# One load of y as two halves on two DMA rings: an elementwise multiply-add on one core

## The chip, the core and the metric

The kernel runs on one NeuronCore of a Trainium2 chip. The metric is device microseconds (us) of one execution, as the median of several. Nearly all of the time goes into transfers by the core's 16 DMA engines (98.6% of the span in the kernel before); two rings feed them in these profiles, one filled by the SP queue (q1) and one by the ACT queue (q10).

Ratios are the mean time of one kernel's fast runs over that of the other's in the same rounds, so they are not quite the ratio of the medians quoted. On one core a run is called slow only because its time is over 1.5% above the fastest of the same kernel.

## The reference

```python
B, S, D = 1024, 16, 512          # bfloat16
def reference(x, y, gamma):      # x, y: (B, S, D); gamma: (D,)
    return x + gamma * y
```

x, y and the output are 16.8 MB each. The 16,384 rows of 512 elements lie as 128 partitions with 128 rows of 1 KB each, so that a load of "rows 0 to 64" moves one contiguous 64 KB run for each of 128 partitions.

## The kernel before

Two lists say what each ring carries, in order. `('y', a, b)` loads rows a to b of y, `('x', a, b, at)` loads rows of x into the x buffer from slot `at`, `('g',)` loads gamma, `('s', a, b)` stores.

```python
PIECES = [53, 11, 53, 11]
SP  = [('y', 0, 64), ('x', 0, 64, 0), ('y', 64, 128), ('x', 64, 117, 0), ('x', 117, 128, 64)]
ACT = [('g',), ('s', 0, 64), ('s', 64, 128)]
EARLY = (1, 0)              # so many of each list are issued ahead of the opening barrier
RELEASE = ('x', 64, 117, 0) # the stores may go once this load has landed
DVE = [('m', 0), ('m', 1), ('a', 0), ('a', 1), ('m', 2), ('m', 3), ('a', 2), ('a', 3)]
# ... cut: buffers; y and the results share one buffer of 128 rows, x has 75 slots ...
def ring(eng, what, n_early):
    known, went = 0, False
    for k, w in enumerate(what):
        kind = w[0]
        need = frees(w) if kind == "x" else ...     # adds that must be over before this goes (cut)
        if need > known:
            eng.wait_ge(s_add, need)
        # ... cut: the DMA itself, with its own semaphore
# gamma is spread over the partitions by a matmul with ones, and cast to bfloat16:
nc.tensor.matmul(gamma_ps, ones_row, gamma_row, start=True, stop=True).then_inc(s_ps, 1)
nc.vector.tensor_copy(out=gamma_sb, in_=gamma_ps).then_inc(s_dve, 1)
# ... cut; then, for each entry of DVE: 'm' is y = y * gamma, 'a' is y = x + y, on one piece of rows
```

The first multiply needs y's first rows **and** gamma. The load `('x', 64, 117, 0)` overwrites slots 0 to 53, so SP holds it back until the first add, of 53 rows, is done. The recorded texts, and so this document, call it "the third x load"; in SP's list it is the second of three, issued together with the third.

## Time and profile before

| | before |
|---|---|
| median of 6 runs | 120.08 us |
| span of the profiled run | 118.6 us |
| share of the span that the 16 engines' packets fill | 66.0 + 32.6 = 98.6% |
| VectorE busy | 70.0 us (59%) |
| matmul that spreads gamma starts | 9.73 us |
| first multiply / first add start | 21.94 / 41.39 us |
| third x load issued | 55.71 us |

The reading order is the shares first, then the timeline; its lines stand in the prediction. The question for every delay is whether it reaches the first point where computing feeds back into the transfers: the third x load. The stores wait for adds too, but with time to spare: the last one is issued at 95.40, and the first one's packets end at 98.3 to 98.9.

### The profile page before, as it was taken

What the parts mean: (1) busy time and instruction counts of PE and PEld (TensorE: products, weight loads), DVE (VectorE), ACT (ScalarE), POOL (GpSimd) and SP (SyncE); (2) the same over time, 40 slices, a digit from 0 to 9 for tenths busy, and PEclk for the clock granted to TensorE, in tenths of its full rate; (3) what the DMA queues carried; (4) which work ended last, traced back from release to release, by engine and by line L of the source; (5) the groups of instructions that cost most, each with busy time, mean ns of one, the idle gap of its engine ahead of it and who ended that gap; (6) DMA issues with size and microseconds to landing.
All of it is one profiled execution on the core that took longest, in us unless ns stands there. A gap on an engine that the chain in (4) does not pass through costs nothing. (4 is left out here: it accounts for less than half of the span.)

```text
span 118.6 us, 78 instructions
## 1 busy us (share of the span) xinstructions
PE 0.6 (0%) x1; PEld 0.1 (0%) x1; DVE 70.0 (59%) x10; POOL 0.2 (0%) x4
## 2 busy tenths in 40 slices
PE   0001000000000000000000000000000000000000
PEld 0000000000000000000000000000000000000000
DVE  0002000599999299999759999999999910000000
POOL 0000000000000000000000000000000000000000
DMA  9889888998899888998896969598899888988892
GB/s 354 354 376 685 354 354 354 597 464 354 354 398 663 354 354 354 663 398 354 354 586 293 586 293 567 220 639 354 354 575 486 354 354 376 685 354 354 354 619 88
DMA packets 1010, 50.33 MB, mean 424 GB/s; under 512 B 113, under 2 KB 114, under 8 KB 114
## 3 DMA queue, kind: packets, MB, share of 16 engines
q1 hardware_dynamic: 720, 33.55, 66.0%
q10 hardware_dynamic: 290, 16.78, 32.6%
HBM read 33.56 MB, written 16.78 MB: 424 GB/s over the span
## 5 line engine op out<-in xcount | busy, mean ns | idle before, releaser
L156 DVE TENSOR_TENSOR y_sb<-y_sb,gamma_sb 128x27136 bf16<-128x27136 bf16 (+1 forms) x4 | 34.6, 8688 | 12.7 <-DVEq L25 12.7
L165 DVE TENSOR_TENSOR y_sb<-x_sb,y_sb 128x27136 bf16<-128x27136 bf16 (+1 forms) x4 | 34.6, 8688 | 2.3 <-DVEq L25 2.2
L132 DVE CAST gamma_sb<-gamma_ps 128x512 bf16<-128x512 f32 x1 | 0.7, 692 | 8.8 <-DVEq L25 8.8
L127 DVE MEMSET ones_row<- 1x128 bf16 x1 | 0.2, 165 | 1.5 <-PEq L41 1.5
L130 PE MATMUL gamma_ps<-gamma_row,ones_row 1*128 1x512 bf16 x1 | 0.6, 578 | 9.7 <-PEq L25 9.7
L130 PEld LDWEIGHTS gamma_ps<-gamma_row,ones_row 1*128 1x128 bf16 x1 | 0.1, 100 | 9.7 <-issue 9.7
L194 POOL MEMSET const-uint8-127<- 128x1 uint8 x1 | 0.1, 102 | 0.0
L194 POOL MEMSET const-bfloat16-1.0<- 128x1 bf16 x1 | 0.1, 101 | 0.0
L194 POOL MEMSET const-float32-0.0<- 128x1 f32 x1 | 0.1, 98 | 0.2 <-issue 0.2
L194 POOL MEMSET const-float32-1.0<- 128x1 f32 x1 | 0.1, 98 | 0.0
## 6 DMA issues: line engine op xcount, KB each, us to landing
x_sb<-in_x_dram SPq DMA_DIRECT2D x1, 6784.0 KB, 20.8
x_sb<-in_x_dram SPq DMA_DIRECT2D x1, 1408.0 KB, 23.9
y_sb<-in_y_dram SPq DMA_DIRECT2D x2, 40.2
out_dram<-y_sb ACTq DMA_DIRECT2D x2, 22.8
x_sb<-in_x_dram SPq DMA_DIRECT2D x1, 39.7
gamma_row<-in_gamma_dram ACTq DMA_DIRECT2D x1, 1.0 KB
```

Source lines behind the costliest of these rows:

```text
L127: nc.vector.memset(ones_row, 1.0).then_inc(s_ones, 1)
L130: nc.tensor.matmul(gamma_ps, ones_row, gamma_row, start=True, stop=True).then_inc(s_ps, 1)
L132: nc.vector.tensor_copy(out=gamma_sb, in_=gamma_ps).then_inc(s_dve, 1)
L156: nc.vector.tensor_tensor(out=yt, in0=yt, in1=g, op=MULT).then_inc(s_dve, 1)
L165: nc.vector.tensor_tensor(out=yt, in0=xt, in1=yt, op=ADD).then_inc(s_add, 1)
L194: nc = _bacc.Bacc("TRN2", target_bir_lowering=False, num_devices=1)
```

## The change

The intent: both rings get work at the earliest moment, and y's first 64 rows come as two halves at once.

```diff
-SP = [('y', 0, 64), ('x', 0, 64, 0), ('y', 64, 128), ('x', 64, 117, 0), ('x', 117, 128, 64)]
-ACT = [('g',), ('s', 0, 64), ('s', 64, 128)]
+SP = [('y', 0, 32), ('x', 0, 64, 0), ('y', 64, 128), ('x', 64, 117, 0), ('x', 117, 128, 64)]
+ACT = [('y', 32, 64), ('g',), ('s', 0, 64), ('s', 64, 128)]

-EARLY = (1, 0)
+EARLY = (1, 1)
```

Gamma's load is not new, but it now stands second in its ring.

## The prediction

> **What bounds the kernel now.** I read the totals first, then the order of instructions, then the waits, then the trace's packet records (one record per transfer of a row by a DMA engine, with queue, start and duration).
>
> ```profile
> span 118.6 us, 78 instructions
> PE 0.6 (0%) x1; PEld 0.1 (0%) x1; DVE 70.0 (59%) x10; POOL 0.2 (0%) x4
> DMA packets 1010, 50.33 MB, mean 424 GB/s; under 512 B 113, under 2 KB 114, under 8 KB 114
> q1 hardware_dynamic: 720, 33.55, 66.0%
> q10 hardware_dynamic: 290, 16.78, 32.6%
> ```
>
> The two queues together fill 66.0 + 32.6 = 98.6% of 16 engines' span; VectorE is busy 59%. The DMA engines are the bound, with bytes that no reordering changes. The span can shrink only out of the 1.4% that is not filled (1.7 us: the start and the last receipt) and can grow only if the engines run dry. Of the packets 896 are data rows (7 large transfers x 128 rows), one is gamma's row of 1 KB, 113 are the small semaphore writes that end each engine's share of a transfer (7 x 16, plus one for gamma, which runs on one engine).
>
> ```profile
> 0.00 0.37 SPq L116 DMA_DIRECT2D y_sb<-in_y_dram  x1
> ...
> 1.43 0.33 SPq L113 DMA_DIRECT2D x_sb<-in_x_dram  x1
> 1.43 0.52 ACTq L110 DMA_DIRECT2D gamma_row<-in_gamma_dram  x1
> ...
> 9.73 0.58 PE L130 MATMUL gamma_ps<-gamma_row,ones_row 1*128 1x512 bf16 x1 [9.73 <-PEq L25]
> 10.46 0.69 DVE L132 CAST gamma_sb<-gamma_ps 128x512 bf16<-128x512 f32 x1 [8.78 <-DVEq L25]
> 21.94 17.29 DVE L156 TENSOR_TENSOR y_sb<-y_sb,gamma_sb 128x27136 bf16<-128x27136 bf16 x2 [10.79 <-DVEq L25]
> 41.39 17.29 DVE L165 TENSOR_TENSOR y_sb<-x_sb,y_sb 128x27136 bf16<-128x27136 bf16 x2 [2.16 <-DVEq L25]
> 55.71 0.81 SPq L113 DMA_DIRECT2D x_sb<-in_x_dram  x2
> 60.63 17.29 DVE L156 TENSOR_TENSOR y_sb<-y_sb,gamma_sb 128x27136 bf16<-128x27136 bf16 x2 [1.95 <-DVEq L25]
> ```
>
> This is the timeline: start, duration, engine, what. Gamma is ready early (cast done 10.46 + 0.69 = 11.15), so the first multiply at 21.94 waits only for y's first 64 rows. The one dependency that feeds back into the DMA stream is at 55.71: the third x load overwrites the x buffer, so SP issues it only when the first add (41.39 + 14.29 for its 53-row piece = 55.68) is done. The packet records show the SP ring still has y rows 64 to 128 to move until 59.6 to 60.0, so this issue is about 4 us early, and the ACT ring is empty then. Each 64 KB packet takes 2.42 us and they follow without a gap from about 1 us on: 16 x 65,536 B / 2.42 us = 433 GB/s.
>
> [...] Gamma was issued at 1.43 while the engine that carries it was on its first y packet (1.01 to 4.41); its 1 KB went at 6.82, between y packets two and three, and its 4-byte semaphore write at 9.28, after the third. [...] gamma, a single row, took 0.52 us when SP's x issue of 0.33 us had begun 5 ns before it. [...]
>
> **The change, part by part.**
>
> Removed: nothing. The same bytes move. The 8.4 MB y load becomes two of 4.2 MB: 128 more packets (32 KB rows instead of 64 KB) and 16 more semaphore writes of about 0.01 us. Cost under 0.1 us per engine. One more semaphore wait on VectorE, about 0.1 us.
>
> Start of the stream: first packets now begin 1.0 to 1.6 us after SP's issue and take 2.7 to 3.4 us instead of 2.42. A second ring can't start before the first did, so I give the start no gain, at most 0.3 us.
>
> Moved: gamma now stands behind y rows 32 to 64 in the ACT ring, and SP's ring goes on with x once its own half is out. Write A1..A8 and B1..B8 for one engine's packets of the halves (1.21 us each), s for a semaphore write, x1.. for x packets (2.42 us). SP issues at 0.00; ACT's first recorded instruction is at 0.13, so I expect [...] one packet committed ahead: A1 A2 B1 A3 B2 ... A8 B7 sA B8 x1 sB x2 gamma x3 sGamma. Sixteen halves take what eight full packets took, so B8 still ends at 21.36 on gamma's engine. Three x packets follow ahead of gamma's semaphore write: 21.36 + 3 x 2.42 = 28.6, and it is seen some 0.3 us later (9.28 to 9.6 before), 28.9. From gamma landed to a multiply able to start is 1.55 us (9.6 to 11.15) plus two waits, 0.2: **30.65 instead of 21.94**, 8.7 us late. y's second half lands near 24.1, no longer the last condition.
>
> How much is absorbed? The multiplies take 17.29: 30.65 + 17.29 + 0.15 (the gap a multiply-to-add wait takes, 77.92 to 78.07) = 48.1 for the first add, which had waited for x until 41.39. It ends at 62.4 and the third x load is issued then, 6.7 us later than 55.71. Its packets follow by at least 1.0 us (the first y load), 63.4; the ring ran dry at 59.6 to 60.0. The engines stand idle some 3.4 to 3.8 us, and the restart stretches the first packet by up to 0.6: **about +4.0 us**.
>
> Does the end take it back? No: x lands 4 us later, the stores start 4 us later, and they fill the DMA engines to the end. Nor does it grow: VectorE then runs unbroken to about 100.2 (48.1 + 3 x 17.29 + 0.15), and the last store, issued there, reaches the engines by about 101.2 to 101.8, ahead of the first store's last packet (98.3 to 98.6 before, 102.4 then).
>
> **Rivals.**
>
> *Even alternation.* If both rings' first packets stand ready together, the order ends A8 B8 sA sB x1 gamma x2 sGamma. Gamma is seen at 21.36 + 2 x 2.42 + 0.3 = 26.5, the multiply starts at 28.3, the third x load is issued at 60.0 and packets resume near 61.1 or later: 1.3 to 1.9 us lost, about 121.7. For it: the halves are small and issued within a fraction of a packet. Against it: [...] the packet committed ahead of gamma.
>
> *ACT gets ahead.* Then its half finishes first, gamma goes in the very next turns, the multiply starts at 22 to 25.5, and the slack of 4 us hides it: 120.1. For it: 0.13 us is little, and ACT's first record then is not a DMA. Against it: SP's issue is the first record of all.
>
> *Deeper commitment.* If what is committed ahead is counted in bytes, two 32 KB packets go before B1, four x packets go before gamma's semaphore write, and all is 2.4 us later: about 126.5. For it: the first store, issued at 76.88, found three or more 11 KB packets still going ahead of it. Against it: the store's own latency may explain that.
>
> *The start gains.* The intent: both rings feeding the engines at once. It would need idle time at the start, of which there is about 1 us before the first packet, set by one issue's latency. I see no way to 2%.
>
> **Range and chances.** SP first with one packet ahead 0.43 (about 124), deeper 0.22 (about 126.5), even 0.19 (about 121.7), ACT first 0.14 (about 120.1), something else 0.02. The 2% line is at 122.5. Slower sums to 0.65, same to 0.33. The median falls on 124.0. The range of 8 in 10 is 120.2 to 126.7.
>
> **What would show each step.** In the changed profile: ACT's y issue near 0.1 to 0.4[...]. The gamma matmul should move from 9.73 to about 29, the first multiply from 21.94 to about 30.7 with the gamma cast just before it, the third x issue from 55.71 to about 62.4, and the DMA row should show a dent of 3 to 4 us near 60 to 64, with nothing idle later. A matmul at 26.6 means even alternation, at 31.4 the deeper commitment, below 24.5 ACT first. The prediction is wrong if gamma slips past the x packets, so that the first add still starts near 41.4, or if the third x load is delayed and the ring nevertheless doesn't run dry.

That one packet goes ahead of a newcomer was the author's estimate, from gamma in the kernel before: issued from 1.43 to 1.95, it went at 6.82, behind a y packet begun at 4.41. The 0.1 us of a semaphore wait was an estimate too; in the runs, the idle time before a first multiply that gamma holds up is 0.37 us with two loads of y to wait for (the changed kernel) and 0.26 with one (one ring, gamma late).

## The result, and the profile after

The changed kernel takes **122.14 us** (121.97 to 122.37, 6 runs) against 120.08: a ratio of 1.0169, with a 95% interval of 1.0153 to 1.0184. It is slower, by less than 2%, which the record's classes call "same".

The totals of the changed kernel's page:

```profile
span 121.1 us, 80 instructions
DMA packets 1154, 50.33 MB, mean 416 GB/s; under 512 B 129, under 2 KB 130, under 8 KB 130
q1 hardware_dynamic: 720, 29.36, 57.5%
q10 hardware_dynamic: 434, 20.97, 40.0%
```

The bytes are those of before. There are 1154 - 1010 = 144 more packets, the 128 of 32 KB and the 16 semaphore writes that were counted beforehand. ACT's ring carries 4.2 MB more.

The timeline of the changed kernel (start, duration, engine, line, what):

```profile
0.00 0.37 SPq L116 DMA_DIRECT2D y_sb<-in_y_dram  x1
0.12 0.38 ACTq L116 DMA_DIRECT2D y_sb<-in_y_dram  x1
...
26.60 0.58 PE L130 MATMUL gamma_ps<-gamma_row,ones_row 1*128 1x512 bf16 x1 [26.60 <-PEq L25]
27.32 0.69 DVE L132 CAST gamma_sb<-gamma_ps 128x512 bf16<-128x512 f32 x1 [25.50 <-DVEq L25]
28.39 17.30 DVE L156 TENSOR_TENSOR y_sb<-y_sb,gamma_sb 128x27136 bf16<-128x27136 bf16 x2 [0.37 <-DVEq L25]
45.83 17.29 DVE L165 TENSOR_TENSOR y_sb<-x_sb,y_sb 128x27136 bf16<-128x27136 bf16 x2
60.15 0.80 SPq L113 DMA_DIRECT2D x_sb<-in_x_dram  x2
63.04 17.29 DVE L156 TENSOR_TENSOR y_sb<-y_sb,gamma_sb 128x27136 bf16<-128x27136 bf16 x2
```

Gamma's matmul starts at 26.60 instead of 9.73, and now it is gamma that the first multiply waits for: the cast ends at 28.01, the multiply starts at 28.39. From there VectorE has no idle time in brackets before any group: everything that had slack (2.16 us before the first add, 1.95 before the second pair of multiplies) is used up. The third x load goes out at 60.15, 4.4 us later than before.

What that does to the transfers is seen in two stretches. First the kernel before, then the changed one; the columns are the stretch, its length, the busy time of PE, PEld, VectorE and POOL with instruction counts, the clock, the DMA share, and GB/s. A packet is counted where it starts.

```profile
59.00:65.00 6.00, 0.00 (x0) 0.00 (x0) 4.37 (x1) 0.00 (x0) 1.00 1.00 434
0.00:59.00 59.00, 0.58 (x1) 0.10 (x1) 35.44 (x6) 0.20 (x4) 1.00 1.00 427
```

```profile
59.00:65.00 6.00, 0.00 (x0) 0.00 (x0) 6.00 (x3) 0.00 (x0) 1.00 0.76 289
0.00:59.00 59.00, 0.58 (x1) 0.10 (x1) 31.32 (x5) 0.20 (x4) 1.00 1.01 427
```

Up to 59 us the two kernels move the same bytes, as far as such a count can tell: it steps by whole packets, of 2.0 to 2.4 us on each engine. No gain of the two rings at the start is seen, and no loss either. Between 59 and 65 us the changed kernel moves (434 - 289) x 6 = 870 KB less, which is one packet of 53 rows less on each of the 16 engines, or **2.0 us** at 434 GB/s.

The packet records show it without such steps. They carry no engine number, but each packet's end meets the next one's start, and so they can be strung into 16 rows. Before, every engine's first packet of the third x load follows its last y packet without a gap, between 59.64 and 60.14, takes 2.00 us, and ends at 61.90 on average. After, the last y packets end at 60.23 to 60.59, the first x packets start at 61.11 to 62.53, most of them take 2.4 to 3.0 us, and they end at 64.02 on average. These 2.1 us are the whole difference of the medians (2.06): on average 0.5 because y itself ended later in this profile, 1.1 of idle time, and 0.5 of a slow first packet. (In the changed kernel's second profile, further down, y ended as before; the idle time was 1.5 and the slow packet 0.7.)

The records also show the order of the packets at the start. Write A1 to A8 for one engine's packets of SP's half, B1 to B8 for those of ACT's half. On all 16 engines the first B packet starts at 2.86 to 3.30 us, directly behind A1, and the rings go on in strict turns; gamma's 1 KB went at 23.61, and its semaphore's last count arrived at 26.46. That is A8 B8, the semaphore writes, one x packet, gamma, another x packet, gamma's semaphore write.

### The profile page after: what moved, and what is told of

The parts are those of the page before. It is cut to its first block, busy times and chain, and to the rows that moved or that the text cites. A ratio compares the mean times of both kernels' runs of the same rounds, so it can differ in the third digit from the quotient of the medians.

```text
span 121.1 us, 80 instructions
## 1 busy us (share of the span) xinstructions
PE 0.6 (0%) x1; PEld 0.1 (0%) x1; DVE 69.9 (58%) x10; POOL 0.2 (0%) x4
## 2 busy tenths in 40 slices
DMA packets 1154, 50.33 MB, mean 416 GB/s; under 512 B 129, under 2 KB 130, under 8 KB 130
## 5 line engine op out<-in xcount | busy, mean ns | idle before, releaser
L130 PE MATMUL gamma_ps<-gamma_row,ones_row 1*128 1x512 bf16 x1 | 0.6, 578 | 26.6 <-PEq L25 26.6
L130 PEld LDWEIGHTS gamma_ps<-gamma_row,ones_row 1*128 1x128 bf16 x1 | 0.1, 100 | 26.6 <-issue 26.6
```

## The experiments

Two theories stood against each other. **Late gamma**: gamma waits behind two of SP's x packets, the first multiply and the first add start late, and the third x load is issued when its ring is already empty. **Two rings**: the second ring with its smaller packets costs time by itself, and gamma's lateness is an accident. A further question was why the packets went in strict turns, and not A1 A2 B1 as the prediction had preferred. Kernels of one batch shared a chip and the runs of the kernel before (medians 119.99, 120.06 and 120.06 us in the three batches).

### Halves kept, gamma moved

```diff
-SP = [('y', 0, 32), ('x', 0, 64, 0), ...
+SP = [('y', 0, 32), ('g',), ('x', 0, 64, 0), ...
-ACT = [('y', 32, 64), ('g',), ('s', 0, 64), ('s', 64, 128)]
+ACT = [('y', 32, 64), ('s', 0, 64), ('s', 64, 128)]
```

> The changed kernel, with gamma's load moved from the ACT ring to the SP ring, right behind SP's half of y and ahead of x; the two halves stay as they are, on two rings at once. Theory 1 (the 2 us come from gamma, which waited behind two x packets, and from nothing else in the two halves): gamma's packet and its semaphore write now go without an x packet ahead of them, near 21.3 us, it is seen near 21.7, the first multiply starts near 23.4, the first add stays at its x-bound 41.4, the third x load is issued near 55.7, nothing runs dry, and the time is that of before within 0.4%: 119.9 to 120.5. Theory 2 (two rings with 32 KB packets cost time by themselves): still 121.5 to 122.5.

Measured: 120.09 us, ratio 1.0011 (0.9994 to 1.0029). Its timeline:

```profile
22.10 0.58 PE L130 MATMUL gamma_ps<-gamma_row,ones_row 1*128 1x512 bf16 x1 [22.10 <-PEq L25]
...
23.89 17.29 DVE L156 TENSOR_TENSOR y_sb<-y_sb,gamma_sb 128x27136 bf16<-128x27136 bf16 x2 [0.37 <-DVEq L25]
41.45 17.29 DVE L165 TENSOR_TENSOR y_sb<-x_sb,y_sb 128x27136 bf16<-128x27136 bf16 x2 [0.27 <-DVEq L25]
55.77 0.81 SPq L113 DMA_DIRECT2D x_sb<-in_x_dram  x2
```

Gamma is still 12 us later than in the kernel before, and the first multiply 2 us later, yet the bracket before the add still holds 0.27 us of idle time: the delay ended there. The halves and both rings are as in the changed kernel, and the loss is gone. "Two rings" falls.

### One ring, gamma late on purpose

```diff
-SP = [('y', 0, 64), ('x', 0, 64, 0), ...                        # the kernel before
+SP = [('y', 0, 64), ('x', 0, 16, 0), ('g',), ('x', 16, 64, 16), ...
-ACT = [('g',), ('s', 0, 64), ('s', 64, 128)]
+ACT = [('s', 0, 64), ('s', 64, 128)]
```

> The kernel before, y's first 64 rows whole on the SP ring, but gamma's load put on the same ring behind the first 16 rows of x (the first x load is cut in two for it). By the packet times 16 rows take 8 x 0.60 = 4.8 us, so gamma is seen near 21.36 + 4.8 + 0.3 = 26.5, as late as in the changed kernel (26.5), with no second ring. Theory 1 (gamma's lateness is the whole cost): matmul near 26.6, first multiply near 28.3, third x issue near 60.1, time 121.8 to 122.5. Theory 2 (the two rings cost it): 119.9 to 120.6.

Measured: 122.06 us, ratio 1.0175 (1.0158 to 1.0192). Timeline, then the stretch around 60 us:

```profile
26.48 0.58 PE L130 MATMUL gamma_ps<-gamma_row,ones_row 1*128 1x512 bf16 x1 [26.48 <-PEq L25]
...
28.16 17.29 DVE L156 TENSOR_TENSOR y_sb<-y_sb,gamma_sb 128x27136 bf16<-128x27136 bf16 x2 [0.26 <-DVEq L25]
...
59.92 0.80 SPq L113 DMA_DIRECT2D x_sb<-in_x_dram  x2
```

```profile
59.00:65.00 6.00, 0.00 (x0) 0.00 (x0) 6.00 (x3) 0.00 (x0) 1.00 0.80 289
```

With one ring and y in one transfer, a gamma as late as in the changed kernel costs the same 2 us in the same place: 289 GB/s again. Here the packet records are cleaner than in the changed kernel: last y packets end at 59.65 to 60.26, first x packets start at 60.87 to 61.32 and take 2.5 to 3.0 us instead of 2.00.

### The same late gamma, with the third x load set free

```diff
-PIECES = [53, 11, 53, 11]
+PIECES = [26, 27, 11, 53, 11]
-SP = [..., ('x', 64, 117, 0), ('x', 117, 128, 64)]
+SP = [..., ('x', 64, 90, 0), ('x', 90, 117, 26), ('x', 117, 128, 64)]
-RELEASE = ('x', 64, 117, 0)
+RELEASE = ('x', 90, 117, 26)
# DVE: m0 m1 m2 a0 a1 a2 m3 m4 a3 a4; the rest is the changed kernel
```

> The changed kernel with its late gamma, but the first 53-row piece is cut into 26 and 27 rows, and so is the third x load, so that its first part waits only for the add of 26 rows. Theory 1 (the lateness costs through the third x load's wait for the first add, which lets the rings run dry): matmul still at 26.6 and the first multiply near 28.4, the first add still near 45.8, but the third x load is issued near 45.9 + 7 = 52.9, 7 us before the ring is empty, no dent near 60, and the time is 119.9 to 120.6. Rival (VectorE itself has become the bound, being busy without a gap from 28 to 98 us): the end still waits for VectorE, 121.7 to 122.6.

> The finer first add once more, to see how often the order of the first packets flips and to get a profile of an execution of its usual time. Where the rings take turns from the first packet (matmul 26.6) the time should be 119.9 to 120.4 with no dent near 60 in the DMA row and the third x load issued near 53; where two packets of SP's half lead (matmul 28.9), 122.2, with the loss not near 60 but near 99, where the last store waits for VectorE. If the loss near 60 had only been moved, the usual time would be over 121.

Measured: 120.08 us in the first batch (three fast runs at 120.04 to 120.12, one slow at 122.21; ratio 1.0005, 0.9988 to 1.0022) and 120.21 us in the second (119.99 to 120.49; ratio 1.0013, 1.0000 to 1.0027). The profile of the second batch, timeline and stretch:

```profile
28.52 17.36 DVE L156 TENSOR_TENSOR y_sb<-y_sb,gamma_sb 128x13312 bf16<-128x13312 bf16 x3 [0.26 <-DVEq L25]
46.03 17.36 DVE L165 TENSOR_TENSOR y_sb<-x_sb,y_sb 128x13312 bf16<-128x13312 bf16 x3
53.15 8.07 SPq L113 DMA_DIRECT2D x_sb<-in_x_dram  x3
```

```profile
59.00:65.00 6.00, 0.00 (x0) 0.00 (x0) 6.00 (x3) 0.00 (x0) 1.00 0.96 413
```

The multiply starts at 28.52 and the add at 46.03, as late as in the changed kernel, but the first part of the third x load goes out at 53.15, and the 2 us are gone. (413 instead of 434 is no sign of a loss: a packet of 26 rows more or less on each engine is 71 GB/s in this count, and the span is 118.9.) So a late first multiply costs nothing by itself, and VectorE, busy without a break from 28.5 us to the end of its work, is not what cost 2 us. That was the issue of the third x load. VectorE has little to spare here, though: its last add ends at 98.04, the last store goes out at 98.07, and the engines stood idle for 0.3 us on average before it (at most 0.76), which they did not in the kernel before.

The slow run of the first batch was the profiled one, and its records show something else. The issues of the two halves stood at 0.00 and 0.13 as always, but the order was A1 A2 B1, on all 16 engines: the first B packet at 3.87 to 4.28. That is the order that the prediction had preferred, and gamma's matmul came at 28.86, where it had put it:

```profile
28.86 0.58 PE L130 MATMUL gamma_ps<-gamma_row,ones_row 1*128 1x512 bf16 x1 [28.86 <-PEq L25]
...
55.17 8.08 SPq L113 DMA_DIRECT2D x_sb<-in_x_dram  x3
```

The third x load was early enough there too; the 2 us more came at the end, where the last store waited for an add that ended at 100.1 and the engines stood idle for 2.0 to 2.8 us. With gamma one x packet later, it was VectorE that the end waited for.

### The changed kernel once more

> The changed kernel unaltered, five more rounds. In its profile the rings took turns from the first packet on (A1 B1 A2 B2 ...), in the profile of the finer first add, with the same issue times, two packets of SP's half went before the first of ACT's (A1 A2 B1 ...). If which of the two comes is settled anew in each execution, some of these runs should take about 2.4 us longer (one x packet): 124.2 to 124.8 beside 122.1. If the order is fixed by the kernel, all lie in 121.9 to 122.5.

Measured: 122.14 us (121.96 to 122.30, 5 runs), ratio 1.0168. No run of 124 appeared, and the profile shows strict turns again (matmul at 26.77). In 11 runs the changed kernel never left its 0.4 us band. Only a profile shows the order itself: of the five profiles with the two halves issued 0.12 us apart, one has A1 A2 B1, that of the finer kernel's slow run; what decides is open.

### Who leads

```diff
-EARLY = (1, 1)
+EARLY = (1, 0)     # ACT's half after the barrier: act_lags
+EARLY = (0, 1)     # SP's half after the barrier: act_leads
```

> The changed kernel, but ACT's half of y is issued after the opening barrier, near 1.5 us, and not at 0.12. Its first packet should be ready near 2.5, while SP's first 32 KB packet runs (1.0 to 2.9). Theory A (one packet is committed ahead of a newcomer, as gamma seemed to show; in the changed kernel the second issue came too early to see it): the order becomes A1 A2 B1 A3 ..., y's second half lands near 24, gamma's matmul moves from 26.6 to about 29.0, the third x issue to about 62.5, time 123.8 to 124.6. Theory B (nothing is committed ahead: strict turns between the rings from the moment both have work): A1 B1 A2 ..., matmul at 26.6 as in the changed kernel, time 121.8 to 122.4. Two committed: matmul near 31.4, time about 126.5.

> The changed kernel with SP's half of y issued after the opening barrier (near 1.5 us) and ACT's at 0.12: the mirror image of the lagging ACT ring, which took 129 us. Theory 1: ACT's half is now the one ahead, by two or three packets, so its ring comes to gamma while SP's ring is still at its own half, no x packet goes before gamma, its matmul starts before 22, the first multiply at 22 to 22.3, and the time is 120.0 to 120.5. Rival (any offset between two rings costs time, whichever leads): 124 or more.

ACT's half lagging: 126.96, 129.09, 129.22 and 129.39 us. The three longer runs count as slow beside the one of 126.96, so no ratio is given, but every one lies 6.97 us or more above the 119.99 of before. The profile (of the 129.09 run):

```profile
1.43 0.39 ACTq L116 DMA_DIRECT2D y_sb<-in_y_dram  x1
...
33.71 0.58 PE L130 MATMUL gamma_ps<-gamma_row,ones_row 1*128 1x512 bf16 x1 [33.71 <-PEq L25]
...
67.25 0.80 SPq L113 DMA_DIRECT2D x_sb<-in_x_dram  x2
```

All three of my numbers were too low for it; the run of 126.96, which has no profile, lies near the 126.5 named for two packets. By the records the first B packet started at 5.23 to 5.38 us on four engines, behind A3, and at 6.51 to 6.82 on the other twelve, behind A4. ACT's issue at 1.43 should have had packets ready near 2.4 to 2.5, had it been as quick as SP's at 0.00 (first packet 0.99). By that estimate two or three packets of 32 KB went ahead of it after the one in progress, not one. The engines then stood idle for over 8 us near 60.

ACT's half leading: 120.11 us, ratio 1.0002 (0.9987 to 1.0017).

```profile
0.13 0.37 ACTq L116 DMA_DIRECT2D y_sb<-in_y_dram  x1
1.58 0.36 SPq L116 DMA_DIRECT2D y_sb<-in_y_dram  x1
...
21.81 0.58 PE L130 MATMUL gamma_ps<-gamma_row,ones_row 1*128 1x512 bf16 x1 [21.81 <-PEq L25]
...
23.60 17.29 DVE L156 TENSOR_TENSOR y_sb<-y_sb,gamma_sb 128x27136 bf16<-128x27136 bf16 x2 [0.37 <-DVEq L25]
...
55.88 0.81 SPq L113 DMA_DIRECT2D x_sb<-in_x_dram  x2
```

The mirror image costs nothing, so it isn't the offset of two rings that costs, but whether gamma's ring is the one behind. Gamma itself went at 20.03, ahead of any x packet; its semaphore write waited a turn longer than I had thought (matmul 21.81, multiply 23.60 instead of 22 to 22.3), within the slack.

### Gamma first, and the half of y late instead

```diff
-ACT = [('y', 32, 64), ('g',), ...
+ACT = [('g',), ('y', 32, 64), ...
-EARLY = (1, 1)
+EARLY = (1, 2)
```

> The changed kernel with gamma ahead of ACT's half in the ACT ring, both issued before the barrier: gamma at 0.12, the half of y near 0.63. Gamma's matmul should start before 9.8. The half lags SP's by about 0.6 us, so one to three of SP's packets lead, and the last packet of ACT's half waits for one or two x packets: y lands near 24.0 to 26.5 and the first multiply starts at 24.1 to 26.6. By the slack of about 4.4 us in the first multiply's start (21.94 to 26.3) that is nearly all absorbed: 119.9 to 120.7. If the first multiply's lateness were not absorbed up to there, 122 or more.

Measured: 121.97 us, ratio 1.0160 (1.0140 to 1.0181). A miss: gamma was there at 4.52, three A packets led, y's second half landed at 26.57 and the multiply started at 26.71, all inside what was expected or 0.1 us beyond it, but the time was not. The third x load was issued at 58.47, over 1 us before the first engine ran out of y packets, and it still cost 1.9 us. By the records most engines went on without a gap, but the first x packets took 2.3 to 3.0 us, and two engines fell 1 us behind the others: their last store packets ended at 120.32 and 120.60, those of the other 14 by 119.22. The span, 121.0, followed the slowest engine. So the slack before the third x issue was smaller than the 4 us I had read off.

### How early the third x load must go

These two are the one-ring kernel with gamma behind 8 and 12 rows of x instead of 16.

> The one-ring kernel with gamma behind 8 rows of x instead of 16, so 2.4 us earlier: matmul near 24.1, first multiply near 25.7, first add near 43.2, third x load issued near 57.5, 2.1 to 2.6 us before the ring is empty. If what counts is that an issue needs 1.0 to 1.6 us to its first packet, nothing is lost: 119.9 to 120.4. If the restart costs more lead than that (gamma_first, issued at 58.47, lost 1.9), 120.6 to 121.5.

> The same with 12 rows: matmul near 25.3, first multiply near 26.9, third x load issued near 58.7, as late as in gamma_first (58.47), but with one ring and y whole. If the lateness of the third x issue alone cost the 1.9 us there, it costs 1.5 to 2.0 here too: 121.5 to 122.1. If it was the lagging half of y on a second ring, little is lost here: 120.0 to 120.7.

Measured: 121.73 us, ratio 1.0149 (1.0125 to 1.0173), with 8 rows; 121.13 us, ratio 1.0085 (1.0072 to 1.0099), with 12. Both matmuls came within 0.4 us of what was expected; both times missed, the first above its two forecasts, the second between them. The 8-row runs spread from 121.33 to 122.13, and the profile is that of the shortest. With 12 rows the late issue alone cost 1.1 us, with an issue later than that of the kernel with gamma first, so 0.8 of the 1.9 us lost there has no cause shown; the lagging half of y is not ruled out for it. Here are the kernels in the order of the third x issue, from their profiles. The kernel with ACT's half lagging (67.25) has no ratio, and the one of the last experiment (57.51) started y 1.7 us late; both are left out.

| kernel | third x issued, us | median, us | ratio to before |
|---|---|---|---|
| finer first add, second batch | 53.15 | 120.21 | 1.0013 |
| before | 55.71 | 120.08 | |
| gamma on SP | 55.77 | 120.09 | 1.0011 |
| ACT leads | 55.88 | 120.11 | 1.0002 |
| one ring, 8 rows | 57.78 | 121.73 | 1.0149 |
| gamma first | 58.47 | 121.97 | 1.0160 |
| one ring, 12 rows | 59.06 | 121.13 | 1.0085 |
| one ring, 16 rows | 59.92 | 122.06 | 1.0175 |
| changed kernel | 60.15 | 122.14 | 1.0169 |

Up to 55.88 nothing is lost; from 57.78 on 1 to 2 us are. The order inside the lower group isn't that of the issue times, and the packet records show two cases.

With the issue at 59.06 or later, the first x packet ended 3.8 to 3.9 us after the issue, as a mean of the 16 engines, in ACT lagging too. In the kernel before it ended at 61.90. An estimate from these numbers, issue + 3.8 - 61.9, gives a loss of 0.96 us (12 rows), 1.82 (16 rows), 2.05 (changed kernel) and 9.15 (ACT lagging). Measured were 1.07, 2.07, 2.06 and, in the profiled run, 9.10.

With the issue at 57.78 and 58.47 the same sum gives nothing and 0.4, but 1.7 and 1.9 were lost. There most engines went on without a gap, yet the first x packets took anything from 2.00 to 2.76 us (8 rows), and the engines ended their last store packets 1.6 us apart (118.02 to 119.64), where before they were 0.6 apart (117.64 to 118.23). So a part of the loss is that of the slowest engine. Why an issue 1 to 2 us ahead of need should upset them is not settled by these runs.

### The length of gamma's issue

```diff
-EARLY = (1, 0)     # the kernel before
+EARLY = (0, 1)     # gamma early and alone; y after the barrier
```

> The kernel before, but gamma is issued on ACT before the barrier, at 0.12, with no other issue beside it, and y's load after the barrier near 1.45. For the length of gamma's issue: [...] if it is what one row costs on the ACT queue, again 0.50. The whole moves with y's issue, 1.4 us later: about 121.5.

Measured: 121.70 us, one run of unknown state. ACT's issue in its timeline:

```profile
0.13 0.52 ACTq L110 DMA_DIRECT2D gamma_row<-in_gamma_dram  x1
```

With no other issue near it, gamma's takes 0.52 us as before: SP's x issue, begun 5 ns ahead of it there, had not lengthened it. In the changed kernel's timeline ACT's half (0.12 to 0.50) overlaps SP's (0.00 to 0.37), and neither is longer than the 0.37 that y's issue took alone in the kernel before, beyond 0.01. With ACT lagging, where SP's x and ACT's half of y were both issued at 1.43, they took 0.33 and 0.39 us.

## Why the prediction was right or wrong

The measured 122.14 lies in the range of 120.2 to 126.7, and the mechanism was the predicted one. That it lies in the range says little: at 6.5 us wide, it holds the times of three of the four packet orders named, and only "ACT first" at 120.1 is outside. And of faster, same and slower at 2%, the likeliest, slower with 0.65, did not come: it is 1.7% slower, in the class given 0.33. The change forecast was +3.9 us, the measured one +2.06.

- **The bound, the bytes, the start.** Right. The same 427 GB/s up to 59 us, 128 + 16 more packets without a visible cost, no gain at the start: y's last half landed at 21.99, the whole before at 21.81.
- **Gamma moved behind y in the ACT ring.** Right, and shown to be the cause from both sides: gamma moved out of there takes the loss away (120.09), gamma made late on one ring brings it back (122.06).
- **The order A1 A2 B1, three x packets ahead of gamma's semaphore write.** This is the step that failed. The changed kernel goes A1 B1, two x packets go ahead, and the multiply starts at 28.39, not 30.65; the term of three packets, 3 x 2.42, measured two. Two grounds had been given. One, on how the two issues go together, was not shown; measured, they overlap (0.00 to 0.37 and 0.12 to 0.50), and gamma's 0.52 us is the same alone. The other, that one packet goes ahead of a newcomer, is not a fixed number: none in the changed kernel's two profiles (first B packets at 2.86 to 3.30 us in the first), one in one profile of the finer kernel with the same issue times (3.87 to 4.28), two or three with ACT's half 1.4 us late (5.23 to 6.82).
- **The even alternation.** This rival had it: matmul 26.6 (measured 26.60), multiply 28.3 (28.39), third x issue 60.0 (60.15), time about 121.7 (122.14). It was given 0.19. The gap that remains is the restart: packets were to resume near 61.1 and did so at 61.48 on average, and the first packet's extra time, put at up to 0.6 us, measured 0.4 to 1.0 on most engines. The prediction's own line on the start, 2.7 to 3.4 us instead of 2.42, holds 0.3 to 1.0.
- **What VectorE adds.** Right: 28.39 + 17.30 + 0.15 = 45.84 (45.83 measured), and nothing more was lost behind it: the last store went out at 97.80, while the first store's last packets ended at 100.4 to 101.4.
- **The slack of 4 us before the third x issue.** Too large. It counted the issue as in time if its first packet could start when the ring ran dry; an issue at 57.78, about 2 us ahead of that, already cost 1.5%. The prediction itself didn't rest on it, since its 62.4 and the measured 60.15 are both beyond, but the expectation for the kernel with gamma first did, and so did the first of the two for 8 rows; both missed.
- **Small readings.** Two ends were read short: y's last packets end by 60.14, not 60.0, and the first store's by 98.9, not 98.6; and 48.1 + 3 x 17.29 + 0.15 is 100.1, not 100.2. Little rests on them: the first makes the idle time 3.3 to 3.8 us.
- **The signs to look for.** The matmul's time told the rivals apart as promised. The dent in the page's DMA row did not show: in slices of 3 us it is lost among slices that alternate between 6 and 9 tenths anyway. Two chosen stretches showed it at once.

## What to carry to other kernels

In these runs the small transfer, gamma, took its place in its ring behind whatever was put there first, and in turns with the large packets of the other ring: its 1 KB went at 6.82 us with nothing ahead of it in its ring, and at 23.61 behind a half of y and one of the other ring's x packets. Before moving a big load onto a second ring, look what small thing stands behind it and what waits for that. Here, where transfers filled 98.6% of the span, a second ring gained nothing (427 GB/s up to 59 us with and without it), and the question about a delay was whether it reached an issue that computing holds back. That issue needed some us of lead: 4 us (issued at 55.71) cost nothing, and about 2 (at 57.78) were not enough (ratio 1.0149). Cutting the piece it waits for in two took this delay off its path (120.21 us), though VectorE then ended just in time for the last store (98.04 and 98.07).
